# One tile of ones instead of two: the tiles on the left of SBUF move by 32 bytes

## The chip, the core and the metric

The kernel runs on one core of a Trainium2 chip. The metric is the device time of one execution in microseconds (us); the time of a kernel is the median of its runs. SBUF, the on-chip memory that the engines read, has 128 partitions. A tile takes the same range of byte addresses in each of them.

## What is computed

The inputs are q, k, v of 6016 x 256, and two pairs of weight matrices of 256 x 2048 and 2048 x 256.

```python
qn = q / (np.linalg.norm(q, axis=1, keepdims=True) + 1e-06)
kn = k / (np.linalg.norm(k, axis=1, keepdims=True) + 1e-06)
s = kn.transpose(0, 2, 1) @ qn / tau            # 256 x 256
a = softmax(s)                                  # over the last axis
x = v @ a                                       # 6016 x 256
x = (s1 * relu(x @ w_in) ** 2 + b1) @ w_out     # first layer
h = x @ w_in2
out = (max(h, 0) + alpha * min(h, 0)) @ w_out2  # second layer
```

q, k and v are float32, and so is the result.

## The kernel before

**Head.** The first 50 us load q and k in 14 pieces, multiply them into two score banks (line 368), square them on ScalarE (lines 350, 353) and sum the squares on VectorE (lines 342, 355, 360). Then comes the softmax of 256 x 256. Its result is multiplied into the first layer's weights (`make_w1`, line 498), so that the first layer works on v directly.

**The two layers.** The 6016 columns are cut into 12 chunks: the first has 480 columns, ten have 512, the last 416. The 2048 hidden units are 16 row blocks, f = 0 to 15. One step t of the main loop (line 695) is one row block of one chunk in each of four stages:

- A (`stage_a`, matmuls at lines 522, 522, 523, 525 in `hidden`): the first layer's hidden units, weights w1h and w1l, moving operands xh and xl. ScalarE applies relu and square; the result is split into a high part g1h and a low part g1l.
- B (`stage_b`, lines 592 to 594): second half of the first layer, weights wo1h and wo1l (w_out), moving operands g1h and g1l.
- C (`stage_c`, `hidden` again): the second layer's hidden units, weights wi2h and wi2l, moving operands yh and yl.
- D (`stage_d`, lines 666 to 668): second half of the second layer, weights wo2, moving operands g2h and g2l.

Each stage has six matmuls per step: high weights times high operand, low times high and high times low, for two halves. Operands are float32 values rounded to the fp32r type, weights are 128 x 128. B follows A by 2 steps, C by 18, D by 19, so that in most steps the four stages work on two chunks. In the last chunk's last steps only C and D are left. Every matmul has its own weight load (PEld in the profile), which TensorE issues while the matmul ahead of it runs.

In the first chunk the high part g1h has two more columns, filled with ones (line 572). Through them w_out's column sums come out in column 480, and line 600 makes the first layer's bias of them.

**Where tiles lie.** Tiles get their addresses when the program is built. Pools on the left are laid out upwards from the constants, pools with `side="right"` downwards from the end of the memory. A tile takes a multiple of 32 bytes in each partition. The left side begins at 16384 with four constants of the framework and the ten small tiles of lines 90 to 99, which take 512 bytes together. All that follow on the left are multiples of 512 bytes long. The addresses in the built program:

| tile | side | begins at | past a multiple of 512 |
|---|---|---|---|
| ones1, ones2, dummy | left | 16800, 16832, 16864 | 416, 448, 480 |
| wraw, wf, vraw (loaded weights and v) | left | from 16896 | 0 |
| xh, xl, yh, yl (moving in A and C) | left | 39424 to 61952 | 0 |
| w1h, w1l, wo1h, wo1l (weights of A, B) | left | 64000 to 113152 | 0 |
| qk, acc, sq (head) | left | 64000 to 147968 | 0 |
| g, g1h, g1l, neg, g2h, g2l, ot | left | 129536 to 160256 | 0 |
| wi2h, wi2l, wo2 (weights of C, D) | right | 163808, 180192, 196576 | 480 |
| wi1, ident, ones, four raw weight tiles (head) | right | 184160 to 213856 | 352 |

Rows of weights are whole multiples of 512 bytes apart: the block for f and half h of w1h begins h x 8192 + f x 512 bytes into the tile.

**What uses the columns of ones.** `ones1` (one column) is the moving operand of two small matmuls at line 392 and the input of a dummy activation at line 323, which loads ScalarE's table early. `ones2` (two columns) is copied at line 572, 16 times.

Of the kernel before, what the change touches and what calls it, by code (L numbers as in the profile page):

```python
# [8 lines left out]
F32 = mybir.dt.float32  # L9
F32R = mybir.dt.float32r  # L10
AF = mybir.ActivationFunctionType
# [35 lines left out]
def tile_channel_attention_mlp_mlp(  # L47
# [18 lines left out]
    nc = tc.nc  # L66
    P = 128
# [18 lines left out]
    const = ctx.enter_context(tc.tile_pool(name="const", bufs=1))  # L86
# [7 lines left out]
    nal_sb = const.tile([P, NF], F32, name="nal_sb")  # L94
    rinv = const.tile([P, NC2], F32, name="rinv")
    bias1 = const.tile([P, NC2], F32, name="bias1")
    ones1 = const.tile([P, 1], F32, name="ones1")
    ones2 = const.tile([P, 2], F32, name="ones2")
    dummy = const.tile([P, 1], F32, name="dummy")

    def bank(tag, name):
        bufs = 2 if tag in ("h1", "h2") else 1
        return ps.tile([P, CH], F32, tag=tag, name=name, bufs=bufs)
# [108 lines left out]
    def run(eng, us, *ready):  # L212
        clk[eng] = max(clk[eng], *ready, 0.0) + us
        return clk[eng]
# [22 lines left out]
    def fill(eng, until):  # L237

        while True:
            while begin():  # L240
                pass
            can = [x for x in active if PARTS[x[2]][0] == eng]
            now = [x for x in can if x[3] <= clk[eng]]
            if not can:
                return
            x = now[0] if now else min(can, key=lambda x: x[3])
            if max(clk[eng], x[3]) + PARTS[x[2]][1] > until + SLIP:
                return
            part(x)
# [34 lines left out]
    with tc.manual_schedule():  # L284
# [17 lines left out]

        nc.vector.memset(ones, 1.0)
        nc.vector.memset(ones1, 1.0)
        nc.vector.memset(ones2, 1.0)
        WM = max(pieces)
        starts = [sum(pieces[:i]) for i in range(NP)]
        qk_t = [
# [11 lines left out]
        for i in range(PIECES_AHEAD):  # L320
            load_piece(i)
        nc.sync.dma_start(tau_sb, tau.partition_broadcast(P))
        nc.scalar.activation(dummy, ones1, AF.Sqrt)
        make_identity(nc, ident)


# [8 lines left out]
        nps = bank("h2", "nps")  # L335
        W = max(t0 + m for t0, m in zip(starts, pieces) if t0 + m <= 8)
        acc = qk.tile([P, 2, W, C], F32, name="acc", bufs=1)
# [52 lines left out]

        for h in range(NC2):
            nc.tensor.matmul(
                nps[:, h : h + 1], acc[:, 1, 0, h * P : (h + 1) * P], ones1,
                start=True, stop=True,
            )
        rq = bank("h2", "rq")
# [121 lines left out]
        def hidden(pt, wh, wl, xhl, f, n):  # L518
            fs = slice(f * P, (f + 1) * P)
            for h in range(NC2):  # L520
                xh = xhl[h][0][:, :n]
                nc.tensor.matmul(pt[:, :n], wh[:, h, fs], xh, start=(h == 0), stop=False)  # L522
                nc.tensor.matmul(pt[:, :n], wl[:, h, fs], xh, start=False, stop=False)  # L523
            for h in range(NC2):
                nc.tensor.matmul(  # L525
                    pt[:, :n], wh[:, h, fs], xhl[h][1][:, :n], start=False, stop=(h == NC2 - 1)
                )

        g1, g2, yps, ops = {}, {}, {}, {}
# [4 lines left out]
        def split_g(g, n, t, nm, on_act):  # L534

            hi = gpool.tile([P, CH], F32R, tag=nm + "h", name=f"{nm}h{t}_{len(g2)}", bufs=GB[nm])
            lo = gpool.tile([P, CH], F32R, tag=nm + "l", name=f"{nm}l{t}_{len(g2)}", bufs=GB[nm])
            if on_act:
                nc.scalar.copy(hi[:, :n], g[:, :n])  # L539

            def rest():
                if not on_act:
                    nc.vector.tensor_copy(hi[:, :n], g[:, :n])  # L543
                nc.vector.tensor_tensor(  # L544
                    lo[:, :n], g[:, :n], hi[:, :n].bitcast(F32), ALU.subtract
                )

            return (hi, lo), rest

        def stage_a(t, on_act):  # L550

            j, f = divmod(t, NF)
            n = chunks[j][1]
            pt = bank("h1", f"h1_{t}")
            hidden(pt, w1h, w1l, xs[j], f, n)
            end = run("pe", 6 * (n * 0.2134 / 512 + 0.0133), at.get(("a", t - 2), 0), state["w1"])
            fill("act", end + 0.2)
            end = run("act", 1.2, end + 0.2)
            g = gpool.tile([P, CH], F32, tag="g", name=f"ga{t}", bufs=3)
            nc.scalar.activation(g[:, :n], pt[:, :n], AF.Relu)  # L560
            nc.scalar.activation(g[:, :n], g[:, :n], AF.Square)  # L561
            at["a", t] = end
            g1[t], rest = split_g(g, n, t, "g1", on_act)
            if on_act:
                end = run("act", 0.55)

            def finish():
                fill("dve", end)
                rest()
                at["g1", t] = run("dve", 0.62 if on_act else 1.05, end)  # L570
                if j == 0:
                    nc.vector.tensor_copy(g1[t][0][:, n : n + 2], ones2)

            return finish

# [201 lines left out]
```

## Time and profile before

| | us |
|---|---|
| median of 3 runs (1130.91 to 1132.38) | 1131.86 |
| the profiled execution | 1130.62 |
| its span | 1128.8 |
| TensorE busy (98% of the span) | 1110.2 |
| VectorE busy (66%) | 741.0 |
| ScalarE busy (49%) | 554.0 |

The profile is of one execution. A start in the timeline is counted from the start of its span. A matmul's duration runs from its start to its modelled end and overlaps the next one's, so the distance between the starts of two matmuls, not the duration, tells how fast TensorE goes on. Weight loads have rows of their own.

### The profile page before, as it was taken

What the parts mean: (1) busy time and instruction counts of PE and PEld (TensorE: products, weight loads), DVE (VectorE), ACT (ScalarE), POOL (GpSimd) and SP (SyncE); (2) the same over time, 40 slices, a digit from 0 to 9 for tenths busy, and PEclk for the clock granted to TensorE, in tenths of its full rate; (3) what the DMA queues carried; (4) which work ended last, traced back from release to release, by engine and by line L of the source; (5) the groups of instructions that cost most, each with busy time, mean ns of one, the idle gap of its engine ahead of it and who ended that gap; (6) DMA issues with size and microseconds to landing.
All of it is one profiled execution on the core that took longest, in us unless ns stands there. A gap on an engine that the chain in (4) does not pass through costs nothing.

```text
span 1128.8 us, 13536 instructions
## 1 busy us (share of the span) xinstructions
PE 1110.2 (98%) x4898; PEld 915.7 (81%) x4898; DVE 741.0 (66%) x1285; ACT 554.0 (49%) x946; POOL 0.7 (0%) x6
## 2 busy tenths in 40 slices
PE   8989999999999999999999999999999999999997
PEld 7857788888888888888888888888888888888897
DVE  3899899756656656665665665665665665665575
ACT  5489987544444444444444444444444444444442
POOL 0000000000000000000000000000000000000000
PEclk9999999999999999999999999999999999999999
DMA  9834242100110020020020020020020010010010
GB/s 357 265 100 106 72 128 63 33 5 1 19 20 1 3 35 1 1 38 1 1 38 1 1 38 1 1 38 1 0 38 1 1 27 8 1 19 1 1 19 16
DMA packets 114627, 42.31 MB, mean 37 GB/s; under 512 B 102784, under 2 KB 103552, under 8 KB 114560
## 3 DMA queue, kind: packets, MB, share of 16 engines
q1 hardware_dynamic: 113696, 39.35, 13.8%
q10 hardware_dynamic: 864, 2.10, 0.5%
q8 instruction: 38, 0.62, 0.2%
q14 instruction: 29, 0.24, 0.1%
HBM read 35.27 MB, written 6.16 MB: 37 GB/s over the span
## 4 chain that ended last, share of the span: by engine, by line
PE 89%; DVE 6%; DMA 2%; ACT 1%; issue 1%; SPq 0%; DVEq 0%; ACTq 0%
PE h L523 15%; PE h L525 15%; PE h L522 15%; PE o L666 8%; PE o L668 8%; PE o L667 8%; PE y L594 7%; PE y L592 7%; PE y L593 7%; DMA qk<-in_k_dram 1%; DVE acc L355 1%; PE wp L498 1%; DMA qk<-in_q_dram 1%; DVE g1l L544 0%; DVE sq L342 0%
## 5 line engine op out<-in xcount | busy, mean ns | idle before, releaser
L642 DVE SCALAR_TENSOR_TENSOR gc<-neg,nal_sb,gc 128x512 f32<-128x512 f32 (+2 forms) x192 | 141.6, 737 | 186.5 <-ACT neg L636 186.2
L635 ACT ACTIVATE gc<-h 128x512 f32<-128x512 f32 (+2 forms) x192 | 113.1, 589 | 265.3 <-PE h L525 251.5
L560 ACT ACTIVATE ga<-h 128x512 f32<-128x512 f32 (+2 forms) x192 | 113.1, 589 | 257.0 <-PE h L525 237.7
L523 PE MATMUL h<-yh,wi2l 128*128 128x512 f32 (+2 forms) x384 | 150.3, 391 | 0.2 <-DVE wi2l L175 0.2
L522 PE MATMUL h<-xh,w1h 128*128 128x512 f32 (+2 forms) x384 | 149.7, 390 | 0.3 <-ACT w1h L507 0.3
L592 PE MATMUL y<-g1h,wo1h 128*128 128x512 f32 (+2 forms) x384 | 148.1, 386 | 1.9 <-ACT wo1h L173 1.7
L522 PE MATMUL h<-yh,wi2h 128*128 128x512 f32 (+2 forms) x384 | 149.5, 389 | 0.4 <-ACT wi2h L173 0.4
L594 PE MATMUL y<-g1l,wo1h 128*128 128x512 f32 (+2 forms) x384 | 149.0, 388 | 0.0
L523 PE MATMUL h<-xh,w1l 128*128 128x512 f32 (+2 forms) x384 | 148.1, 386 | 0.5 <-DVE w1l L511 0.5
L593 PE MATMUL y<-g1h,wo1l 128*128 128x512 f32 (+2 forms) x384 | 147.9, 385 | 0.2 <-DVE wo1l L175 0.2
L666 PE MATMUL o<-g2h,wo 128*128 128x512 f32 (+2 forms) x368 | 144.4, 392 | 0.5 <-DVE g2h L543 0.5
L667 PE MATMUL o<-g2h,wo 128*128 128x512 f32 (+2 forms) x368 | 144.1, 391 | 0.0
L668 PE MATMUL o<-g2l,wo 128*128 128x512 f32 (+2 forms) x368 | 143.3, 390 | 0.0
L544 DVE TENSOR_TENSOR g1l<-ga,g1h 128x512 fp32r<-128x512 f32 (+2 forms) x192 | 130.6, 680 | 16.5 <-ACT g1h L539 1.6
L544 DVE TENSOR_TENSOR g2l<-gc,g2h 128x512 fp32r<-128x512 f32 (+2 forms) x184 | 126.2, 686 | 17.1 <-PE h L525 0.5
L543 DVE CAST g1h<-ga 128x512 fp32r<-128x512 f32 (+1 forms) x158 | 66.5, 421 | 90.9 <-ACT ga L561 90.0
L561 ACT ACTIVATE ga<-ga 128x512 f32<-128x512 f32 (+2 forms) x192 | 119.7, 623 | 6.1
L525 PE MATMUL h<-yl,wi2h 128*128 128x512 f32 (+2 forms) x384 | 119.0, 390 | 0.0
L525 PE MATMUL h<-xl,w1h 128*128 128x512 f32 (+2 forms) x384 | 116.6, 385 | 0.0
L636 ACT ACTIVATE neg<-h 128x512 f32<-128x512 f32 (+2 forms) x192 | 112.3, 585 | 0.0
L543 DVE CAST g2h<-gc 128x512 fp32r<-128x512 f32 (+2 forms) x184 | 78.0, 424 | 16.9 <-DVE gc L642 0.5
L592 PEld LDWEIGHTS y<-g1h,wo1h 128*128 128x128 f32 x384 | 72.1, 188 | 16.5 <-ACT wo1h L173 2.1
(107 smaller groups left out, 1281.6 us busy)
## 6 DMA issues: line engine op xcount, KB each, us to landing
vraw<-in_v_dram SPq DMA_DIRECT2D x80, 64.0 KB, 2.5
out_dram<-ot SPq DMA_DIRECT2D x80, 64.0 KB, 1.9
qk<-in_q_dram SPq DMA_DIRECT2D x7, 640.0 KB, 11.1
wi1r<-in_moe_w_in_dram SPq DMA_DIRECT2D x8, 512.0 KB, 7.5
wo1r<-in_moe_w_out_dram SPq DMA_DIRECT2D x8, 512.0 KB, 4.0
wi2r<-in_moe_w_in_dram SPq DMA_DIRECT2D x8, 512.0 KB, 3.6
wo2r<-in_moe_w_out_dram SPq DMA_DIRECT2D x8, 512.0 KB, 3.7
qk<-in_k_dram SPq DMA_DIRECT2D x5, 640.0 KB, 11.7
```

Source lines behind the costliest of these rows:

```text
L522: nc.tensor.matmul(pt[:, :n], wh[:, h, fs], xh, start=(h == 0), stop=False)
L523: nc.tensor.matmul(pt[:, :n], wl[:, h, fs], xh, start=False, stop=False)
L525: nc.tensor.matmul(pt[:, :n], wh[:, h, fs], xhl[h][1][:, :n], start=False, stop=(h == NC2 - 1))
L543: nc.vector.tensor_copy(hi[:, :n], g[:, :n])
L544: nc.vector.tensor_tensor(lo[:, :n], g[:, :n], hi[:, :n].bitcast(F32), ALU.subtract)
L592: nc.tensor.matmul(yp[:, :m], wo1h[:, f, cs], hi[:, :m], start=(f == 0), stop=False)
L593: nc.tensor.matmul(yp[:, :m], wo1l[:, f, cs], hi[:, :m], start=False, stop=False)
L594: nc.tensor.matmul(yp[:, :n], wo1h[:, f, cs], lo[:, :n], start=False, stop=(f == NF - 1))
L642: nc.vector.scalar_tensor_tensor(g[:, :n], neg[:, :n], nal_sb[:, f : f + 1], g[:, :n], op0=ALU.mult, op1=ALU.add,)
L666: nc.tensor.matmul(op, wo2[:, f, 0, cs], hi, start=(f == 0), stop=False)
L667: nc.tensor.matmul(op, wo2[:, f, 1, cs], hi, start=False, stop=False)
L668: nc.tensor.matmul(op, wo2[:, f, 0, cs], lo, start=False, stop=(f == NF - 1))
```

## The change

`ones1` becomes two columns wide, `ones2` is gone with its memset, and the three uses take `ones1` or its first column. The small tiles take 480 bytes instead of 512 together. So every tile on the left that comes after them begins 32 bytes lower, 480 bytes past a multiple of 512; the tiles on the right stay where they were. No other instruction is added, removed or moved on any engine.

```diff
--- before.py
+++ after.py
@@ -94,8 +94,7 @@
     nal_sb = const.tile([P, NF], F32, name="nal_sb")
     rinv = const.tile([P, NC2], F32, name="rinv")
     bias1 = const.tile([P, NC2], F32, name="bias1")
-    ones1 = const.tile([P, 1], F32, name="ones1")
-    ones2 = const.tile([P, 2], F32, name="ones2")
+    ones1 = const.tile([P, 2], F32, name="ones1")
     dummy = const.tile([P, 1], F32, name="dummy")
@@ -302,7 +301,6 @@
 
         nc.vector.memset(ones, 1.0)
         nc.vector.memset(ones1, 1.0)
-        nc.vector.memset(ones2, 1.0)
         WM = max(pieces)
         starts = [sum(pieces[:i]) for i in range(NP)]
         qk_t = [
@@ -320,7 +318,7 @@
         for i in range(PIECES_AHEAD):
             load_piece(i)
         nc.sync.dma_start(tau_sb, tau.partition_broadcast(P))
-        nc.scalar.activation(dummy, ones1, AF.Sqrt)
+        nc.scalar.activation(dummy, ones1[:, :1], AF.Sqrt)
         make_identity(nc, ident)
 
 
@@ -390,7 +388,7 @@
 
         for h in range(NC2):
             nc.tensor.matmul(
-                nps[:, h : h + 1], acc[:, 1, 0, h * P : (h + 1) * P], ones1,
+                nps[:, h : h + 1], acc[:, 1, 0, h * P : (h + 1) * P], ones1[:, :1],
                 start=True, stop=True,
             )
         rq = bank("h2", "rq")
@@ -569,7 +567,7 @@
                 rest()
                 at["g1", t] = run("dve", 0.62 if on_act else 1.05, end)
                 if j == 0:
-                    nc.vector.tensor_copy(g1[t][0][:, n : n + 2], ones2)
+                    nc.vector.tensor_copy(g1[t][0][:, n : n + 2], ones1)
 
             return finish
```

## Rows read from the trace of the kernel before

**Rows 1.** The page: TensorE's busy time and share; its granted clock in 40 slices.

```profile
PE 1110.2 (98%) x4898; PEld 915.7 (81%) x4898; DVE 741.0 (66%) x1285; ACT 554.0 (49%) x946; POOL 0.7 (0%) x6
...
PEclk9999999999999999999999999999999999999999
```

**Rows 2.** The waits, longest in total: who waited for whom, us, times, longest.

```profile
ACT gc L635 <- PE h L525: 251.5, 176, 2.8
```

**Rows 3.** Timeline of TensorE, one steady step: start us, us, line, operation, tiles.

```profile
503.83 0.39 PE L522 MATMUL h<-xh,w1h 128*128 128x512 f32 x1
...
505.19 0.39 PE L592 MATMUL y<-g1h,wo1h 128*128 128x512 f32 x1
...
506.56 0.39 PE L522 MATMUL h<-yh,wi2h 128*128 128x512 f32 x1
...
507.96 0.39 PE L666 MATMUL o<-g2h,wo 128*128 128x512 f32 x1
...
509.35 0.39 PE L522 MATMUL h<-xh,w1h 128*128 128x512 f32 x1
```

**Rows 4.** Groups by shape, all the span: count, then busy us and mean ns.

```profile
L522 PE MATMUL h<-yh,wi2h 128*128 128x512 f32 x320 | 126.0, 394 | 0.0
...
L522 PE MATMUL h<-xh,w1h 128*128 128x512 f32 x320 | 124.6, 389 | 0.0
```

**Rows 5.** Weight loads grouped, 205 to 985 us: count, busy us, mean ns.

```profile
L522 PEld LDWEIGHTS h<-xh,w1h 128*128 128x128 f32 x284 | 53.3, 188 | 11.7
...
L522 PEld LDWEIGHTS h<-yh,wi2h 128*128 128x128 f32 x282 | 52.8, 187 | 12.0
```

**Rows 6.** Timeline of VectorE at the program's start: the memset removed.

```profile
0.96 0.06 DVE L305 MEMSET ones<- 128x2 f32 x1
```

**Rows 7.** Timeline of TensorE: A and B have 416 columns, C and D 512.

```profile
1005.67 0.35 PE L522 MATMUL h<-xh,w1h 128*128 128x416 f32 x1
...
1007.91 0.40 PE L522 MATMUL h<-yh,wi2h 128*128 128x512 f32 x1
...
1010.72 0.35 PE L522 MATMUL h<-xh,w1h 128*128 128x416 f32 x1
```

**Rows 8.** Timeline of TensorE: A and B have 512 columns, C and D 480.

```profile
201.95 0.39 PE L592 MATMUL y<-g1h,wo1h 128*128 128x512 f32 x1
...
203.32 0.38 PE L522 MATMUL h<-yh,wi2h 128*128 128x480 f32 x1
...
205.96 0.40 PE L522 MATMUL h<-xh,w1h 128*128 128x512 f32 x1
```

**Rows 9.** Timeline of TensorE, first chunk: A alone with B, 480 columns.

```profile
108.37 0.38 PE L522 MATMUL h<-xh,w1h 128*128 128x480 f32 x1
...
109.69 0.38 PE L592 MATMUL y<-g1h,wo1h 128*128 128x482 f32 x1
```

**Rows 10.** Timeline of TensorE, the tail: C and D alone, 416 columns.

```profile
1095.14 0.35 PE L522 MATMUL h<-yh,wi2h 128*128 128x416 f32 x1
...
1096.26 0.35 PE L666 MATMUL o<-g1h,wo 128*128 128x416 f32 x1
```

**Rows 11.** Line 175, VectorE's subtraction: count, ns min/median/max, starts.

```profile
L175 DVE TENSOR_TENSOR wo1l<-wo1f,wo1h x8: 681/684/694, 72.0 to 105.6; 128x512 fp32r<-128x512 f32 x8
L175 DVE TENSOR_TENSOR wi2l<-wi2f,wi2h x8: 682/685/693, 118.1 to 202.4; 128x512 fp32r<-128x512 f32 x8
```

**Rows 12.** Line 126's loads issued at 69.0 and 71.2 us, then at 98.6.

```profile
DMA to landing us min/median/max: 3.6/3.9/4.2
...
DMA to landing us min/median/max: 3.6/3.6/3.6
```

**Rows 13.** The chain of work that ended last: start us, us, what.

```profile
9.82 11.35 DMA qk<-in_k_dram
```

**Rows 14.** Timeline of TensorE: A has 512 columns, B still 480 and 482.

```profile
118.88 0.40 PE L522 MATMUL h<-xh,w1h 128*128 128x512 f32 x1
...
120.27 0.38 PE L592 MATMUL y<-g1h,wo1h 128*128 128x482 f32 x1
```

## Prediction

> **What bounds the kernel now.** I read the page's busy shares first, then the waits, and then the timeline of TensorE, which is where this change can act. TensorE is busy 98% of the span, with the clock at 0.9 or more in all 40 slices, so the upper of its two levels, 2.4 GHz [rows 1]. The largest wait of the whole program is ScalarE waiting for stage C's matmuls: 251.5 us in 176 waits [rows 2]. So in the two layers, which fill most of the span, the time is the number of matmuls times the distance from the start of one to the start of the next. I call that distance the pitch.
>
> The reader is to see the pitch in the start column of the timeline. One step of the steady part has 24 matmuls of 512 columns, six in each of the stages A, B, C and D. A starts at 503.83, B at 505.19, C at 506.56, D at 507.96 and the next A at 509.35 [rows 3]. That gives A 1.36, B 1.37, C 1.40 and D 1.39 us, and 5.52 us for the step. All four do the same work: fp32r, 128x128 weights, 512 columns. Yet A and B take 1.36 / 6 = 0.227 us for one matmul, and C 1.40 / 6 = 0.233. The durations grouped by shape say the same: 389 ns for A's first line, 394 for C's over 320 matmuls each [rows 4]. A duration in that view runs over into the next matmul, so only differences count. The weight loads do not differ: 188 ns in A, 187 in C [rows 5]. What differs is the address. Weights of A and B begin at a multiple of 512 bytes, those of C and D 480 past one, and all moving tiles at a multiple. From one row block to the next the weights' address moves by 512 or 1024 bytes, so the 320 matmuls of one mean [rows 4] hold all multiples; what C's have in common against A's is the remainder, or the side of the memory.
>
> **What the change does, part by part.** One memset goes (0.06 us of VectorE at 0.96 us [rows 6]). TensorE's warm-up matmuls, which wait for the last memset, may start that much earlier. But the first data that the chain of work waits for is a load in flight then, and VectorE's work waits for that load, so I take 0.
>
> Everything else is addresses. The left tiles move from remainder 0 to 480; those on the right stay. In C and D, weights and moving operand had remainders 480 and 0 and now have 480 and 480. In A and B they had 0 and 0 and now have 480 and 480. My forecast is that **the difference of the two remainders sets the pitch**, since the next weights are loaded while the current operand streams: a load of 188 ns [rows 5] lies inside every pitch of 0.227 us, so both are read from the same memory at once. Then A and B, whose difference is 0 before and after, stay at 1.36, and C and D fall to it. Three steps of the sum:
> - Steps in which all four stages have 512 columns. A runs two steps ahead of B and 18 ahead of C, and D one behind C, so these are t = 34 to 175, 142 steps. Each falls from 5.52 to 4 x 1.36 = 5.44 us, so 142 x 0.08 = 11.4 us.
> - 18 steps with 416 columns in A and B and 512 in C and D. A with B take 1007.91 - 1005.67 = 2.24, C with D 1010.72 - 1007.91 = 2.81 [rows 7]. If C and D fall to 2.72, that is 18 x 0.09 = 1.6; if the change of length disturbs them, 0. I take 1.2.
> - 18 steps with 512 columns in A and B and 480 in C and D. There C with D take 205.96 - 203.32 = 2.64, 1.32 each [rows 8]. Stage A with 480 columns and equal remainders also took 109.69 - 108.37 = 1.32 [rows 9]. So at 480 columns the relation is worth next to nothing, and I take 0.4 for these steps and 0 for the first 16, where only A and B run.
>
> The tail, where C and D run alone with 416 columns, gains nothing: C takes 1096.26 - 1095.14 = 1.12, or 0.187 a matmul [rows 10], which is just the weight load of 187 to 188 ns [rows 5]. A and B at that length take 2.24 together, also 0.187 [rows 7]. So there the loads stand end to end, and they are no slower from remainder 480 than from 0. That is the main reason why I do not put the 6 ns on the weights' own address.
>
> What could be lost elsewhere: the vector engines and the loads. VectorE's subtraction takes a median 684 ns into w_out of the first layer (remainder 0) and 685 into wi2 (480) [rows 11], so nothing. For loads, the nearest rows are two blocks into right-hand tiles (remainder 352), landing in 3.6 to 4.2 us, and one into a left tile (0), in 3.6 us [rows 12]. That bounds the loss at 0 to 15% of a load. Only the first pieces of q and k lie on the end's path (one of 11.35 us [rows 13]); the rest come behind VectorE's sums. Between 0 and 1.7 us I take 0, because loads that start together share the engines and a lone one shows no loss. In the Trainium skill, "DMA: Bandwidth & Descriptors", section "How a descriptor splits into AXI transactions", a rule speaks against this change: a descriptor that does not begin at a multiple of 256 bytes needs one transaction more. By it a 5 KB row would need 21 instead of 20, an estimate of 5%, and the sum would lose some 0.6 us; the rows show no clear sign of it.
>
> Sum: 11.4 + 1.2 + 0.4 = 13.0 us. Against the profiled execution (1130.62 us) that is 1117.6; the median of the runs is 1131.86, which I start from, so **1118.9 us**. With only the first term it is 1120.5. With the second at 1.6 and 0.05 us in the mixed steps of 480 columns it is 1117.9, and 1116.5 leaves room for the first chunk and the runs' spread. With the 1.7 us of loads the upper end is about 1122. Next in line after TensorE nothing is late: C's results are waited for by ScalarE, not the other way round [rows 2].
>
> **Rivals.**
> 1. *Slower: the weights' own remainder costs.* Then A and B, whose weights now begin 480 past a multiple too, rise to 1.40, and C and D stay. A step becomes 5.60, so 142 x 0.08 = 11.4, and with A and B of 512 columns 2 x 0.03 slower in the 18 mixed steps 1.1 more: 1131.9 + 12.5 = 1144.4. It decides if the pitch with equal remainders of 480 is above 0.230. For it: in the trace weights at 480 always go with the slow pitch at 512 columns. Against it: at 416 and at 480 columns they do not [rows 7 to 10]. 11 in 100.
> 2. *Slower: equal remainders do not settle.* Stage A at 512 columns and equal remainders once took 120.27 - 118.88 = 1.39, when B between had 482 columns [rows 14], so 0.227 is a rhythm that has to be reached. After 480-column stages it was reached within a step: B takes 203.32 - 201.95 = 1.37 [rows 8]. If it is lost, a step is 4 x 1.39 = 5.56, or 0.04 x 142 = 5.7 more: 1137.6. 8 in 100, as 24 equal matmuls disturb less than what it recovers from now.
> 3. *The moving operand's own remainder costs.* No fp32r row has one off 0. From below it is bounded by no loss, which is the forecast; from above by 0.0067 us on each of the 24 on top of C's pitch, 5.76 a step, 142 x 0.24 = 34: about 1166. 4 in 100.
> 4. *Nothing moves: the side of the memory counts, or the change does not reach the cause.* C and D differ from A and B in lying on the right too, and no row separates this from the remainder. Then 1131.9. Against it: at 416 columns the right is as fast as the left [rows 7, 10]. 13 in 100. In the Trainium skill, "TensorE: Matmul & The Clock Gate", section "Step-by-step: what each phase is for", TensorE has two independent read ports, and the next weights' load takes nothing from the running matmul. By that rule no remainder would matter and the sum would be 0; the trace does not agree as it stands, with 0.227 and 0.233 for equal work [rows 3].
>
> **How the numbers follow.** The forecast has 64 in 100, the rivals 11, 8, 4 and 13. About 0.2% (2.3 us) is what a measurement of this kernel can tell from no change. Faster is the forecast, 0.64; same is rival 4, 0.13; slower is rivals 1 to 3, 0.23. From 1116.5 to 1138 lie the forecast, rival 4 and rival 2, together 85, less a few for sizes that I miss, so 8 in 10. The forecast's own range is 1116.5 to 1122.
>
> **What would show it.** In the timeline of the changed kernel, around 500 us, starts of A, B, C, D should be 1.36 apart each and a step 5.44; by rival 1 1.40 and 5.60, by rival 2 1.39 and 5.56, by rival 4 unchanged at 1.36, 1.37, 1.40, 1.39. Grouped by shape, C's matmuls should read 389 ns as A's do, where now they read 394 [rows 4]. VectorE's and ScalarE's durations and the tail's 1.12 should stay. A step of 5.52 with other times inside, or a loss before 60 us of more than 1.7, would make the prediction wrong.

## The result

The changed kernel takes 1118.62 us (median of 4 runs, 1118.45 to 1118.93), the kernel before 1132.12 in the same comparison (1130.91 to 1133.26). The ratio is 0.9881 with a 95% interval of 0.9864 to 0.9898, so it is faster by 1.2%, 13.5 us. The profiled executions, which the rows come from, differ by 11.9: 1130.62 to 1118.72, spans 1128.8 to 1116.9.

TensorE is still the bound: it is busy 98% of a shorter span. From the page of the changed kernel:

```profile
PE 1098.7 (98%) x4898; PEld 917.0 (82%) x4898; DVE 740.5 (66%) x1284; ACT 553.8 (50%) x946; POOL 0.7 (0%) x6
...
PEclk9989999999999999999999999999999999999999
```

The steady step, in TensorE's timeline (start us, duration us, line, operation, tiles), answers to [rows 3]:

```profile
500.27 0.39 PE L520 MATMUL h<-xh,w1h 128*128 128x512 f32 x1
...
501.63 0.39 PE L590 MATMUL y<-g1h,wo1h 128*128 128x512 f32 x1
...
502.99 0.39 PE L520 MATMUL h<-yh,wi2h 128*128 128x512 f32 x1
...
504.35 0.39 PE L664 MATMUL o<-g2h,wo 128*128 128x512 f32 x1
...
505.71 0.39 PE L520 MATMUL h<-xh,w1h 128*128 128x512 f32 x1
```

A, B, C and D are now 1.36 us apart each, and the step is 505.71 - 500.27 = 5.44, where it was 5.52. In this step nothing but C and D and the crossing from B to C became shorter. Grouped by shape over the whole span (count, then busy us and mean ns), the answer to [rows 4]:

```profile
L520 PE MATMUL h<-xh,w1h 128*128 128x512 f32 x320 | 124.6, 389 | 0.0
...
L520 PE MATMUL h<-yh,wi2h 128*128 128x512 f32 x320 | 124.6, 389 | 0.0
```

C's matmuls went from 394 to 389 ns, A's stayed at 389. Two starts of A, 142 steps apart, tell what this is worth in all. In the trace of before, the first is at 222.31 and the second is the first of [rows 7], at 1005.67:

```profile
222.31 0.39 PE L522 MATMUL h<-xh,w1h 128*128 128x512 f32 x1
```

In the changed kernel the same two are at

```profile
222.83 0.39 PE L520 MATMUL h<-xh,w1h 128*128 128x512 f32 x1
```

```profile
994.83 0.35 PE L520 MATMUL h<-xh,w1h 128*128 128x416 f32 x1
...
997.07 0.39 PE L520 MATMUL h<-yh,wi2h 128*128 128x512 f32 x1
...
999.79 0.35 PE L520 MATMUL h<-xh,w1h 128*128 128x416 f32 x1
```

Before, 783.36 us lay between them, now 772.00, so 11.4 us were gained there. The last three rows answer to [rows 7]: A with B 2.24 as before, C with D 2.72 instead of 2.81.

### The profile page after: what moved, and what is told of

It is laid out like the page before. It is cut to its first block, busy times and chain, and to the rows that moved or that the text cites. A ratio compares the mean times of both kernels' runs of the same rounds, so it can differ in the third digit from the quotient of the medians.

```text
span 1116.9 us, 13535 instructions
## 1 busy us (share of the span) xinstructions
PE 1098.7 (98%) x4898; PEld 917.0 (82%) x4898; DVE 740.5 (66%) x1284; ACT 553.8 (50%) x946; POOL 0.7 (0%) x6
## 4 chain that ended last, share of the span: by engine, by line
PE 89%; DVE 7%; DMA 2%; ACT 1%; issue 1%; ACTq 0%; DVEq 0%; SPq 0%
PE h L521 15%; PE h L523 15%; PE h L520 15%; PE o L666 8%; PE o L664 8%; PE o L665 7%; PE y L590 7%; PE y L591 7%; PE y L592 7%; DMA qk<-in_k_dram 2%; DVE acc L353 1%; PE wp L496 1%; DVE g1l L542 0%; DVE sq L340 0%; DVE wi L163 0%
## 5 line engine op out<-in xcount | busy, mean ns | idle before, releaser
L664 PE MATMUL o<-g2h,wo 128*128 128x512 f32 (+2 forms) x368 | 142.7, 388 | 0.5 <-DVE g2h L541 0.5
L665 PE MATMUL o<-g2h,wo 128*128 128x512 f32 (+2 forms) x368 | 142.4, 387 | 0.0
L523 PE MATMUL h<-yl,wi2h 128*128 128x512 f32 (+2 forms) x384 | 116.7, 385 | 0.0
L521 PEld LDWEIGHTS h<-xh,w1l 128*128 128x128 f32 x384 | 72.8, 190 | 15.6 <-issue 1.0
```

The source lines that it names most:

```text
L523: nc.tensor.matmul(pt[:, :n], wh[:, h, fs], xhl[h][1][:, :n], start=False, stop=(h == NC2 - 1))
L664: nc.tensor.matmul(op, wo2[:, f, 0, cs], hi, start=(f == 0), stop=False)
L665: nc.tensor.matmul(op, wo2[:, f, 1, cs], hi, start=False, stop=False)
```

## Experiments: is it the addresses, and which of them?

The kernels differ only in unused tiles that shift others (one in a slice). A step is read around 500 us, as above. Times with one run are single executions and tell some us, not tenths.

**undo32** is the changed kernel with 32 unused bytes behind the small tiles:

```diff
     dummy = const.tile([P, 1], F32, name="dummy")
+    pad = const.tile([P, 8], F32, name="pad")
```

> The kernel after with an unused tile of 32 bytes behind the small tiles: every address is that of before again, one memset is still gone. If the addresses carry the gain: 1131 to 1133 us, a step at 500 us of 5.52 with C 1.40 and D 1.39. If the missing memset or another trifle of the head carried it: 1118 to 1120.

Measured: 1132.24 us (median of 10 runs), ratio to before 1.0002, interval 0.9992 to 1.0012. Its step is that of before: 1.37, 1.40, 1.39, 1.36 from B on. The starts of B, C, D, A and B:

```profile
500.92 0.39 PE L591 MATMUL y<-g1h,wo1h 128*128 128x512 f32 x1
...
502.29 0.39 PE L521 MATMUL h<-yh,wi2h 128*128 128x512 f32 x1
...
503.69 0.39 PE L665 MATMUL o<-g2h,wo 128*128 128x512 f32 x1
...
505.08 0.39 PE L521 MATMUL h<-xh,w1h 128*128 128x512 f32 x1
...
506.44 0.39 PE L591 MATMUL y<-g1h,wo1h 128*128 128x512 f32 x1
```

So the 32 bytes carry the gain, and the missing memset is worth nothing beyond the 0.1% of the interval. (Of the small tiles `dummy` alone stays 32 bytes lower.)

**right0** leaves the left side of before alone and moves the right side to remainder 0:

```diff
                 wdst["wo2"] = w2pool.tile([P, NF, 2, C], F32R, name="wo2")
+                w2pool.tile([P, 120], F32, name="pad2")
```

> The kernel before, left side untouched (remainder 0), the weights of C and D moved down by 480 bytes to remainder 0. Theory, the difference of the remainders sets the pitch: all stages 1.36, step 5.44, 1117 to 1120 us. Rival, moving operands have to lie at 480 for C and D to be fast: step 5.52, 1132 us.

Measured: 1118.16 us (median of 4 runs), ratio to before 0.9876, interval 0.9859 to 0.9892. B, C, D and the next A start at

```profile
501.27 0.39 PE L592 MATMUL y<-g1h,wo1h 128*128 128x512 f32 x1
...
502.63 0.39 PE L522 MATMUL h<-yh,wi2h 128*128 128x512 f32 x1
...
503.99 0.39 PE L666 MATMUL o<-g2h,wo 128*128 128x512 f32 x1
...
505.35 0.39 PE L522 MATMUL h<-xh,w1h 128*128 128x512 f32 x1
```

B, C and D are 1.36 long (and A, which began at 499.91). Equal remainders of 0 do what equal remainders of 480 do, so neither value is good or bad by itself. It is as fast as the changed kernel (the intervals overlap), and no kernel here beats both.

**w480** and **m480w0** make the remainders unequal in all four stages. The first moves the weights of A and B (kernel before), the second starts from the changed kernel and moves all weights to 0, with moving operands at 480:

```diff
 w480, in before
+        w1pool.tile([P, 120], F32, name="pad0")
         w1h = w1pool.tile([P, NC2, F], F32R, name="w1h")
...
         wo1l = w1pool.tile([P, NF, C], F32R, name="wo1l")
+        w1pool.tile([P, 8], F32, name="pad1")
 m480w0, in after
+        w1pool.tile([P, 8], F32, name="pad0")
         w1h = w1pool.tile([P, NC2, F], F32R, name="w1h")
...
         wo1l = w1pool.tile([P, NF, C], F32R, name="wo1l")
+        w1pool.tile([P, 120], F32, name="pad1")
...
                 wdst["wo2"] = w2pool.tile([P, NF, 2, C], F32R, name="wo2")
+                w2pool.tile([P, 120], F32, name="pad2")
```

> The kernel before with the weights of A and B moved up by 480 bytes on the left, moving operands at 0 as before; now all weights are at 480 and all moving operands at 0. Theory of the difference: A and B rise to 1.39 or 1.40, step 5.57 to 5.60, 1142 to 1145 us. Rival, the side of the memory slows C and D: A and B stay at 1.36, 1132 us.

> All moving operands at remainder 480, all weights at 0, on both sides: the difference of before's C and D with the sign turned, in all four stages. Theory of the difference by 64: all stages 1.39 to 1.40, step 5.57 to 5.60, 1142 to 1146 us. Rival, moving operands at 480 are fast whatever the weights: step 5.44, 1119 us. Rival, weights at 0 are fast whatever the moving operands: step 5.44, 1119 us.

Measured: 1144.60 and 1144.43 us (one run each). The starts of C, D, A and B in w480:

```profile
501.26 0.39 PE L524 MATMUL h<-yh,wi2h 128*128 128x512 f32 x1
...
502.66 0.39 PE L668 MATMUL o<-g2h,wo 128*128 128x512 f32 x1
...
504.06 0.39 PE L524 MATMUL h<-xh,w1h 128*128 128x512 f32 x1
...
505.46 0.39 PE L594 MATMUL y<-g1h,wo1h 128*128 128x512 f32 x1
...
506.86 0.39 PE L524 MATMUL h<-yh,wi2h 128*128 128x512 f32 x1
```

Every stage takes 1.40, the step 5.60. A and B, on the left, became as slow as C and D were, so the side of the memory is out. In m480w0 the weights lie at 0 and the moving operands at 480, and it is as slow, so neither operand's own remainder decides. Its step, from one start of C to the next, is 5.60 too:

```profile
501.07 0.40 PE L522 MATMUL h<-yh,wi2h 128*128 128x512 f32 x1
...
506.67 0.40 PE L522 MATMUL h<-yh,wi2h 128*128 128x512 f32 x1
```

From the worst case to the best (right0) it is 26 us for the same instructions.

In all these kernels the tiles that ScalarE and VectorE work on in the two layers share the remainder of the moving operands, so a clash of the weight loads with those two engines would move with the addresses in the same way. The trace of w480 speaks against it. Between 230 and 960 us there are 103 matmuls with both engines idle for more than three quarters of the time to the next start, and their mean pitch is 0.233 us. It is 0.233 as well for the 2091 matmuls during which one or the other was busy all the time.

**How finely do the addresses count?** In five kernels the weights of C and D take other remainders, moving operands at 0. The edit is that of right0 with 56 (d256), 88 (d128), 104 (d64), 112 (d32) or 64 (d224) columns instead of 120. A sixth, d16, puts them 16 bytes past a multiple of 256 through a slice:

```diff
-                    w2pool.tile([P, NC2, F], F32R, name=f"wi2{x}") for x in "hl"
+                    w2pool.tile([P, NC2 * F + 64], F32R, name=f"wi2{x}")[
+                        :, 4 : 4 + NC2 * F
+                    ].rearrange("p (a f) -> p a f", a=NC2)
+                    for x in "hl"
...                                                   (wo2 in the same way)
```

> The kernel before with the weights of C and D at remainder 256 and the moving operands at 0: a difference of 256. If the two have to agree within all 512 bytes: C and D near 1.40, step about 5.52, 1131 to 1133 us. If addresses repeat every 256 bytes or less: step 5.44, 1117 to 1120 us.

> The kernel before with the weights of C and D at remainder 128, moving operands at 0. A difference of 256 was as fast as none. If addresses repeat every 64 or 128 bytes: step 5.44, 1117 to 1120 us. If only every 256: C and D near 1.40, 1131 to 1133.

> The same with remainder 64. If addresses repeat every 64 bytes: step 5.44, 1117 to 1120 us. If every 128 or 256: C and D near 1.40, 1131 to 1133.

> The same with remainder 32; before it was 480, which is 32 short of a multiple. If only the difference by 64 counts, 32 and 480 are the same case: C and D 1.40 and 1.39, 1131 to 1133 us. If the sign of the difference counts: another step, between 5.44 and 5.60.

> The kernel before with the weights of C and D at remainder 224 instead of 480, moving operands at 0. If addresses count by 256 bytes, 224 and 480 are the same case: C 1.40, D 1.39, step 5.52, 1131 to 1133 us, matmul for matmul as before. If 0 and 256 are special for another reason: another step.

> The kernel before with the weights of C and D 16 bytes past a multiple of 256 (a slice that begins 4 elements into a longer tile), moving operands at 0. If only whole units of 32 or 64 bytes count: step 5.44, 1117 to 1120 us. If the two starts have to be equal within 256 bytes to the 16 bytes: C and D 1.39 to 1.40, 1130 to 1136.

Starts are printed to 0.01 us, so a stage's time may be 0.01 off.

| kernel | remainder of C's and D's weights | one run, us | A, B, C, D, us |
|---|---|---|---|
| right0 | 0 | 1118.16 (median) | 1.36, 1.36, 1.36, 1.36 |
| d16 | 16 past a multiple of 256 | 1121.29 | 1.36, 1.37, 1.36, 1.35 |
| d32 | 32 | 1132.42 | 1.37, 1.37, 1.39, 1.40 |
| d64 | 64 | 1135.26 | 1.39, 1.36, 1.40, 1.40 |
| d128 | 128 | 1136.33 | 1.39, 1.37, 1.39, 1.40 |
| d224 | 224 | 1134.27 | 1.36, 1.37, 1.40, 1.39 |
| d256 | 256 | 1119.42 | 1.36, 1.36, 1.36, 1.36 |

The differences 0 and 256 are fast and 32, 64, 128 and 224 slow. 224 has the step of 480, stage for stage. So these addresses count by 256 bytes, not by 512 as I had put it, and not by 32, 64 or 128 bytes, which the expectations had left open. Four of the six times fell outside the ranges expected. d64 and d128 are above 1133 because A was slow too, which makes their steps 5.55. d224 is 2.5 us above before on the same chip though its step is the same; its one execution was late in the head (the A of t = 16 starts at 121.50, in the profile of before at 118.88) and slow in the tail (2.32 us a step, in before 2.24). d16, at 1121.29, lies between its two cases: 16 bytes are near enough to 0 in the steady part, but d16 does not gain where the lengths differ. Two starts of A that follow each other, with 416 columns in A and B:

```profile
995.32 0.35 PE L522 MATMUL h<-xh,w1h 128*128 128x416 f32 x1
...
1000.37 0.35 PE L522 MATMUL h<-xh,w1h 128*128 128x416 f32 x1
```

That is 5.05 for the step, as before (1010.72 - 1005.67 [rows 7]), against 4.96 in the changed kernel (999.79 - 994.83).

d64 brought something that I had not expected. Its rows of A, B, C, D and the next A:

```profile
500.65 0.39 PE L522 MATMUL h<-xh,w1h 128*128 128x512 f32 x1
...
502.04 0.39 PE L592 MATMUL y<-g1h,wo1h 128*128 128x512 f32 x1
...
503.40 0.40 PE L522 MATMUL h<-yh,wi2h 128*128 128x512 f32 x1
...
504.80 0.40 PE L666 MATMUL o<-g2h,wo 128*128 128x512 f32 x1
...
506.20 0.39 PE L522 MATMUL h<-xh,w1h 128*128 128x512 f32 x1
```

A's operands were not touched and have equal remainders, yet A takes 1.39. So it does in d128.

**c0d480** tests how the stages add up. Only C's weights go to remainder 0; D's stay at 480:

```diff
+                w2pool.tile([P, 120], F32, name="pad2")
                 wdst["wo2"] = w2pool.tile([P, NF, 2, C], F32R, name="wo2")
```

> The kernel before with the weights of C alone moved to remainder 0, those of D left at 480. Theory: a matmul's pitch goes by its own moving operand and the weights loaded meanwhile, which are the next matmul's. Then B falls to 1.36 (its last matmul is followed by a load of C's weights), C is 1.36 and a little, D stays at 1.39: step 5.47 to 5.49, 1123 to 1127 us. Rival, the pitch goes by a matmul's own weights: B stays at 1.37 and D at 1.39 to 1.40.

Measured: 1132.52 us (one run), against 1131.75 for before on the same chip. The starts of A, B, C, D and A:

```profile
500.11 0.40 PE L522 MATMUL h<-xh,w1h 128*128 128x512 f32 x1
...
501.50 0.39 PE L592 MATMUL y<-g1h,wo1h 128*128 128x512 f32 x1
...
502.86 0.39 PE L522 MATMUL h<-yh,wi2h 128*128 128x512 f32 x1
...
504.23 0.39 PE L666 MATMUL o<-g2h,wo 128*128 128x512 f32 x1
...
505.63 0.40 PE L522 MATMUL h<-xh,w1h 128*128 128x512 f32 x1
```

C fell to 1.37, as my theory had it. B reads 1.36 here and 1.37 in the next step (507.01 to 508.38), so B does not tell theory and rival apart. D took 1.40, and A rose from 1.36 to 1.39, so the step is 5.52 as before and half of the cure is worth nothing. The sum of 5.47 to 5.49 was missed.

Which weights count, a matmul's own or the next one's, can be read in the kernel before. Line 594 runs twice in stage B, and the second time the next weights are C's. Line 668 runs twice in stage D, and the second time the next weights are A's. Lines 593 and 667 always have weights of their own stage next. Their durations in ns (min/median/max), 230 to 960 us:

```profile
L593 PE MATMUL y<-g1h,wo1l x265: 389/389/389, 230.1 to 958.7; 128*128 128x512 f32 x133
...
L594 PE MATMUL y<-g1l,wo1h x266: 389/392/396, 229.6 to 959.0; 128*128 128x512 f32 x133
...
L667 PE MATMUL o<-g2h,wo x264: 393/394/396, 232.2 to 956.0; 128*128 128x512 f32 x132
...
L668 PE MATMUL o<-g2l,wo x264: 389/392/394, 232.4 to 956.2; 128*128 128x512 f32 x132
```

B's sixth matmul is slow (396; in the step of [rows 3] it is the one at 506.33) though its own two remainders are equal, and D's sixth is fast (389) though its own differ. So there the next weights count, as the theory says and its rival does not. Elsewhere the theory still fails. In c0d480 D's last matmul has A's weights next, with equal remainders, and takes 505.63 - 505.39 = 0.24. In d64 B takes 1.36, though its last matmul has C's weights next, with unequal ones. A matmul's pitch is not a function of one pair of remainders alone, whichever weights one takes. After D's last matmul in c0d480, A is slow for a whole stage with equal remainders, as [rows 14] had shown beside another neighbour. In the kernel before, D itself took 1.39 and A went on at 1.36. What makes the difference stays open.

## Why the prediction was right, and where its parts were off

**The main term held.** 142 steps x 0.08 = 11.4 us, and 11.4 were measured. The reading behind it was that equal work at two pitches [rows 3] has to come from addresses, and that what counts is the difference between moving operand and next weights, not one operand's own remainder. right0, w480 and m480w0 bear that out. The rule is narrower than I wrote it: the remainders count by 256, they need not be equal to the byte, and a neighbour can spoil a stage whose own are equal (d64, d128, c0d480).

**The smaller terms.** The 18 steps with 416 columns gave 18 x 0.09 = 1.6, not 1.2: unequal lengths did not disturb the rhythm here. The steps with 480 columns in C and D gave more than the 0.4 that I took. They are 16, not 18, because C begins only at t = 18. From B's start to the next A's it was 205.96 - 201.95 = 4.01 [rows 8], and now it is 206.69 - 202.73 = 3.96:

```profile
202.73 0.39 PE L590 MATMUL y<-g1h,wo1h 128*128 128x512 f32 x1
...
204.09 0.38 PE L520 MATMUL h<-yh,wi2h 128*128 128x480 f32 x1
...
206.69 0.39 PE L520 MATMUL h<-xh,w1h 128*128 128x512 f32 x1
```

C with D take 2.60 instead of 2.64 and B 1.36 instead of 1.37. Over all 16 steps, from the A of t = 18 (124.28 before, 125.66 now) to that of t = 34 (211.33 and 212.01), it is 0.7 us. My evidence was stage A at 1.32 [rows 9], but with B of 482 columns beside it, and that is not the same neighbour. The tail, which I held at 0, was 0.4 us longer from the first C of 416 columns to the end. C now takes 1093.04 - 1091.91 = 1.13 and D 1.13, where C took 1.12 [rows 10]:

```profile
1091.91 0.35 PE L520 MATMUL h<-yh,wi2h 128*128 128x416 f32 x1
...
1093.04 0.35 PE L664 MATMUL o<-g1h,wo 128*128 128x416 f32 x1
...
1094.17 0.35 PE L520 MATMUL h<-yh,wi2h 128*128 128x416 f32 x1
```

This cannot be put on the change, for in undo32, with the addresses of before, a step of the tail takes 2.32, where it is 2.24 in before and 2.26 in the changed kernel:

```profile
1117.46 0.35 PE L521 MATMUL h<-yh,wi2h 128*128 128x416 f32 x1
...
1119.78 0.35 PE L521 MATMUL h<-yh,wi2h 128*128 128x416 f32 x1
```

So the tail's pitch is not simply the weight load's 187 ns, as I had read it from [rows 10]. With that, both grounds that I gave against rival 1 are weak: at 480 columns the addresses do count, and at 416 the pitch varies while the addresses stay. The forecast held, but the experiments show it and not these two grounds.

**The loads and VectorE held.** The six second-layer loads from 95 to 125 us land in 3.5 to 4.3 us with left tiles at 480 (3.5 to 4.5 before, medians 3.6), the first number of each row being the minimum:

```profile
DMA to landing us min/median/max: 3.5/3.6/4.3
```

The rule on transactions of 256 bytes in the Trainium skill, "DMA: Bandwidth & Descriptors", section "How a descriptor splits into AXI transactions", would have had to show here if it holds for the SBUF end of a load, since these tiles moved from a multiple of 256 to 224 past one. The trace shows no cost. The large load of [rows 13] takes 11.21 now, and 11.35 before. My bound on the loads was a little low: 4.2 us over 3.6 [rows 12] is 17%, not 15%. VectorE's subtraction into w_out of the first layer, now at remainder 480, takes a median of 686 ns, where it took 684 [rows 11].

**What I did not foresee is in the head, and undo32 has a part of it too.** In the profiled execution of the changed kernel, the A that started at 99.70 us before starts at 101.09, 1.4 us later. The windows of 66 to 70 us (length, busy us of PE, PEld, DVE, ACT, POOL, granted clock, DMA's share and GB/s) show a difference that fits. After, before, and undo32, which has the addresses of before:

```profile
66.00:70.00 4.00, 3.77 (x9) 2.80 (x10) 4.00 (x9) 3.56 (x7) 0.00 (x0) 0.50 0.79 253
```

```profile
66.00:70.00 4.00, 3.49 (x16) 2.74 (x15) 4.00 (x10) 3.94 (x8) 0.00 (x0) 1.00 0.63 238
```

```profile
66.00:70.00 4.00, 3.38 (x9) 2.42 (x9) 4.00 (x9) 3.60 (x7) 0.00 (x0) 0.57 0.73 248
```

The granted clock is 0.50 in the first, the lower level of 1.2 GHz, 1.00 in the second and 0.57 in the third. TensorE was idle for part of the stretch ahead in all three (4.18, 4.19 and 4.32 us busy of the 6 from 60 to 66 us). undo32 shows that the lower clock comes without the shift too. In the changed kernel most of the loss arises there: the first A starts 0.2 us later than before (64.66 against 64.46), the first B 1.4 us later (73.41 against 72.02). So 11.4 + 1.6 + 0.7 - 0.4 = 13.3 is what the steps gained; less the 1.4 that is 11.9, as between the spans. The medians differ by 13.5. Against the forecast of 13.0 the underestimated small terms make it a little more. That 1118.9 came within 0.3 us of 1118.62 is in part luck, since the head's clock and the tail's pitch, neither of which I had in the sum, each move a single execution by 1 us or more.

**The rivals.** Rival 1 (the weights' own remainder) would have given 1144.4 and fell with the changed kernel; its step of 5.60 is that of w480, where the remainders are unequal everywhere. Rival 2 (equal remainders that do not settle) did not happen in this change, but its mechanism is real: A at 1.39 in d64, d128 and c0d480. Rival 3 and the unchanged time of rival 4 fell with the changed kernel, and the side of the memory with w480. The rule that stood beside rival 4 (the Trainium skill, "TensorE: Matmul & The Clock Gate", section "Step-by-step: what each phase is for": two independent read ports, so that a weight load takes nothing from the running matmul) cannot stand as it is for these fp32r matmuls, since by it no remainder would matter. Moving the weights by some hundred bytes moves the same program from 1118 to 1144 us, while the loads' own duration, 187 to 188 ns [rows 5], did not tell fast from slow.

**What stays open.** That the stream of the moving operand and the load of the next weights meet in the memory fits most rows (not A in d64, d128 and c0d480, nor D's last matmul in c0d480 and B's in d64), but it was argued, not shown. No run looked at a matmul without a load beside it. Nor is it known why the pitch settles at 0.227 and not lower.

## What to carry to other kernels

When equal matmuls run at two pitches in one trace, compare the addresses of their operands before anything else. Here moving operands and next weights that begin alike within 256 bytes gave 0.227 us for 512 columns, unless a neighbour spoiled it, and others about 0.233, and 32 bytes of small tiles decided between them. Align all stages at once, since curing one of two neighbours gained nothing. Take the pitch from start to start at the length that the kernel runs, because at 416 columns, with 0.187 us a matmul and weight loads of 187 to 188 ns, A with B took 2.24 in both kernels and C's and D's pitch did not follow the remainders.

## What the runs showed that I had not expected

- A matmul's pitch depends on those that ran before it: stage A, untouched and with equal remainders, took 1.36 us in the kernel before and 1.39 in c0d480, d64 and d128.
- At 512 columns differences of 0, 16 and 256 bytes are fast; 32, 64, 128, 224 and 480 are slow.
- From 66 to 70 us the granted clock was 1.00 in before and 0.57 in undo32, which has the same addresses. In the changed kernel it was 0.50, and the first B came 1.4 us late, about as much as the larger of the small terms.
- The 13 runs of before beside undo32 follow their mean granted clock: 1129.62 us at 0.999, 1134.18 at 0.994.
